# A long convolution and an MLP in one kernel: the engine and the place of batch 0's intermediate stores

## The chip, the core and the metric

One core of one Trainium2 chip runs the whole kernel. The metric is device microseconds of one execution; before the change the median of three runs is 1598.55 us (1595.64 to 1606.63).

## What is computed

The reference is a gated long convolution (sequence 12480, 128 channels, batch 2) followed by a two-layer MLP with a leaky ReLU:

```python
h_filt = (np.maximum(pos_emb @ w1, 0.0) @ w2) * np.exp(-0.01 * pos)[:, None]
u = x * v
Hf = np.fft.rfft(h_filt, n=L, axis=0)            # L = 2 * S
y = np.fft.irfft(np.fft.rfft(u, n=L, axis=1) * Hf[None], n=L, axis=1)[:, :S, :]
t = (x * y).reshape(B * S, D)
h = t @ w_in                                     # 128 -> 2048
out = np.maximum(0.01 * h, h) @ w_out            # 2048 -> 128
```

## The kernel before

The transform is cut as 98 times 128 points, so that each part is a matmul. The work has three stages, and on each engine the instructions run in the order in which the program writes them (`manual_schedule`).

**First stage** (to about 142 us; lines 265 to 409). For 16 groups of positions SyncE loads the transform's factors, x and v; TensorE does the 98-point transform of batch 0 and of the filter's hidden layer; the results go to the DRAM scratch `scr1`. Every DMA of this stage is started by SyncE.

**Second stage** (about 142 to 312 us; lines 697 to 885), batch 0. A loop over 25 chunks of four frequencies each (`KC` = 4, `NCH` = 25; the last frequency chunk has two) goes in the order `ORD`: chunks 13 to 24, then 12, then 0 to 11. Below, i is the place in this order, and "chunk 18" means i = 18. Iteration i does:

- `load_b` (line 705): SyncE loads the data of chunk i+3 (768 KB, four buffers `bin`);
- matmuls `hp` (line 846), and two ScalarE copies into `hs` (line 850): the filter's spectrum of this chunk (tile `hs`, two buffers);
- `fwd` (line 135): the forward transform `up`; then `hidden(i+1)` (line 790), copied by ScalarE into `es` (line 793);
- `store_h` (line 815): two DMAs of 256 KB that put `hs` into the DRAM scratch `hspec`, from where batch 1's work reads it in the third stage (`fetch_h`, line 489). ScalarE starts them;
- up to five steps of `weights` (line 708): eight rounds of three iterations turn the float64 weights into pairs of float32r. Integer work on VectorE (lines 80 to 91) reads the raw tiles `wi64` and `wo64`; the next round's loads (lines 717 and 718, 256 KB each) stand in iterations 3, 6, ..., 21, and the first instruction that reads the loaded tile (line 80) comes in the same iteration, behind the product;
- `product` (lines 143 and 144): four VectorE multiplications of `up` with `hs` and two sums, one of them on GpSimd (in the last two iterations both on VectorE);
- for chunk i-1: the back transform `dp` (line 163), two ScalarE copies into `ct` (line 238; two buffers), and `store_back` (line 220): one DMA of 512 KB to the scratch `scr2`, started by ScalarE (for the last chunk by SyncE). For the last two chunks `last_c` (line 657) also copies four short rows straight from `ct` into `cin[0]`, the input of the third stage's first tile.

Also in this loop, on SyncE: `first_c` (reads of `scr2` for tile 0) in iterations 15 to 19; `fetch_a(0)` and `fetch_a(1)` (lines 246 to 256: seven DMAs, 1.4 MB, for batch 1's first transform) in iterations 20 and 23; `load_gx(0)` and `load_gx(1)` (lines 605 to 620, six DMAs) in iterations 23 and 24; `rows_c` (line 650) in iteration 24, which reads rows of `scr2` up to those of chunk 22. `mult_a` (line 262) multiplies what `fetch_a` brought, on GpSimd.

Behind the loop come `ahead(1)` (four steps of `conv`, the generator of batch 1's transforms, whose first step stands before the loop), the rest of `weights`, the last chunk's back transform, and `join_hi(0)`, `upper_c(1)` and `rows_c(1, ...)`: the loads of tile 1's `cin`.

**Third stage** (to the end; lines 888 to 1248). Tiles of 390 positions of the output are joined, back-transformed, gated and put through the MLP, in 49 blocks of 16 steps (`NF` = 16); batch 1's transforms (`conv`) run between. `steps` is a table written out before the loop: at step i of the third stage, `do` runs what is due there ("piece" at step 2, "mult" at 9, loads and joins by the tables `gets` and `turn_at`). Join work of tile 1 is due at steps 2 to 4. Pools `s0` (tags s0, s1: three buffers each) and `sc` (tag s4: two buffers) are used from the first stage to the third by `fetch_a`, by batch 1's chunks and by `conv`'s output `o1`.

A DMA is started by an instruction on the queue of SyncE (SPq) or of ScalarE (ACTq); in the views it is a row DMA_DIRECT2D of that queue, and while it waits, everything behind it on the same engine waits too.

Of the kernel before, what the change touches and what calls it, by code (L numbers as in the profile page):

```python
# [8 lines left out]
F32 = mybir.dt.float32  # L9
# [21 lines left out]
def tile_conv_mlp(ctx, tc, x, v, pos_emb, w1, w2, w_in, w_out, cf, cr, cg, cb, ci, cw, out):  # L31
# [78 lines left out]
    def run(g):  # L110
        for _ in g:
            pass
# [105 lines left out]
    def store_back(b, c, ct, eng):  # L218
        k0, n = chunk(c)
        eng.dma_start(out=scr2[b][k0:k0 + n].rearrange("k r m e -> (r m) k e"),  # L220
                          in_=ct[:, :n].rearrange("p k s d -> p k (s d)"))
# [20 lines left out]
    with tc.manual_schedule():  # L242
# [175 lines left out]
        wc_l = wp.tile([128, D], F32R, name="wc_l")  # L418
        sc = ctx.enter_context(tc.tile_pool(name="sc", bufs=2, reuse_waits="tile"))
        psc = {}  # L420
        N1 = HB // MC1
        WAIT = 12
        PRE = 2
# [273 lines left out]
        with ExitStack() as st:  # L697
# [97 lines left out]
            def evac(c):  # L795
                ct = sbb.tile([128, KC, 2, D], F32, tag="ct", name="ct", bufs=2)
                k0, n = chunk(c)
                end = c == ORD[-1]
                dp = dps.pop(c)
                if end:  # L800
                    for s, copy in ((0, nc.scalar.copy), (1, nc.vector.tensor_copy)):
                        copy(ct[:, :n, s, :], dp[s][:, :n * D].rearrange("p (k d) -> p k d", d=D))
                else:
                    run(back_evac(dp, ct, n))
                if c in ORD[-2:]:
                    last_c(ct, k0, n, [nc.sync] * 3 + [nc.scalar if end else nc.sync])
                store_back(0, c, ct, nc.sync if end else nc.scalar)

            def store_h(c, hs, i):

                w = chunk(c)[1] * D

                def put(eng):
                    for s in range(2):
                        eng.dma_start(out=hspec[c][:, :, s, :w], in_=hs[HB * s:HB * s + HB, :, :w])
                put(nc.scalar)

            eh, dps = {}, {}
            first_c = upper_c(0)
            ahead(A0)  # L820
            next(conv)
            hidden(ORD[0])
            for i, c in enumerate(ORD):
                if i + 3 < NCH:
                    load_b(ORD[i + 3])
                if NCH - 10 <= i < NCH - 5:
                    next(first_c)
                if i == NCH - 2:
                    load_gx(0)
                if i == NCH - 1:  # L830
                    load_gx(1)
                    rows_c(0, 0, 0, (MID - 2) * KC)
                if i in FETCH:
                    fetch_a(FETCH.index(i))
                if i == NCH - 2:
                    mult_a(0)
                for f in late:
                    f()
                late = []
                n = chunk(c)[1]  # L840
                t, es = bins.pop(c), eh.pop(c)
                hp = two("h")
                for ri in range(2):
                    for k in range(n):
                        h, j = 64 * (k % 2), ri * n // 2 + k // 2
                        nc.tensor.matmul(hp[k % 2][:, D * j:D * j + D], es[h:h + 64, k // 2, ri, :], w22[h:h + 64, :],
                                         start=True, stop=True)
                hs = sbb.tile([128, 2, KC // 2, 2, D], F32, tag="hs", name="hs", bufs=2)
                for k in range(2):
                    nc.scalar.copy(hs[:, :, :n // 2, k, :],  # L850
                                   hp[k][:, :n * D].rearrange("p (r j d) -> p r j d", r=2, d=D))
                hs = hs.rearrange("p r j i d -> p r (j i d)")
                up = two("u")
                fwd(up, lambda s: t[:, :n, s, FO:], n)
                if i + 1 < NCH:
                    hidden(ORD[i + 1])
                store_h(c, hs, i)
                for _ in range(3):
                    next(wprep, None)
                pins[c] = sbb.tile([128, 2, 512], F32, tag="pin", name="pin", bufs=2)  # L860
                ab = [sbb.tile([128, 2, 512], F32, tag=g, name=g) for g in ("ta", "tb")]
                product(ab, up, hs, n * D, pins[c], nc.vector if i >= NCH - 2 else nc.gpsimd)
                if i >= 1:
                    b4 = ORD[i - 1]
                    dps[b4] = two("d")
                    back_halves(dps[b4], pins.pop(b4), b4)
                    evac(b4)
                for _ in range(2):
                    next(wprep, None)

            def flush():
                for f in late:
                    f()
                late.clear()

            ahead(1)
            run(wprep)
            mult_a(1)
# [1 line left out]
            back_halves(dps[ORD[-1]], pins.pop(ORD[-1]), ORD[-1])  # L880
            evac(ORD[-1])
            run(join_hi(0))
            run(upper_c(1))
            rows_c(1, 0, 0, KH)
            psc["held"] = []
# [278 lines left out]
                at(0, "load", t)  # L1164

        at(2, "piece", 0)
        at(9, "mult", PRE)

        def do(what, t, i):
            if what == "piece":  # L1170
                run(pieces_out.pop(0))
                for f in psc.pop("held"):
                    f()
                fetch_a(PRE)
            elif what == "mult":
                mult_a(t)
            elif what == "conv":
# [139 lines left out]
```

## Time and profile before

| | us |
|---|---|
| median of three runs | 1598.55 |
| the runs | 1598.55, 1595.64, 1606.63 |
| the profiled execution | 1601.6 |
| its span | 1599.7 |
| TensorE busy (matmuls) | 1555.3 (97%) |
| VectorE busy | 1138.7 (71%) |
| ScalarE busy | 998.1 (62%) |
| GpSimd busy | 767.0 (48%) |

The span is what the profiler saw between the first and the last instruction; the execution's own time has 1.9 us more around it. Times in the rows are counted from the span's start. Shares of the whole span say little here, as the three stages have different limits, and only the second stage and its end are touched by the change.

### The profile page before, as it was taken

How to read it: one execution, taken by the hardware profiler on the slowest of the kernel's cores; microseconds unless marked ns; L12 is line 12 of the kernel's file. 1: busy time of each engine (PE TensorE's matmuls, PEld its weight loads, DVE VectorE, ACT ScalarE, POOL GpSimd, SP SyncE). 2: the span in 40 equal slices, each digit the busy share in tenths (PEclk: the TensorE clock that was granted, in tenths of full speed). 3: DMA queues.
4: the chain of work that ended last, by engine and by line, in shares of the span. 5: the costliest groups of instructions: out<-in, count | busy, mean ns of one | idle time of the engine just before them, and what ended most of it. 6: DMA issues, size and time to landing. Idle time of an engine off the chain costs nothing.

```text
span 1599.7 us, 27485 instructions
## 1 busy us (share of the span) xinstructions
PE 1555.3 (97%) x9241; PEld 1322.6 (83%) x9241; DVE 1138.7 (71%) x1785; ACT 998.1 (62%) x2108; POOL 767.0 (48%) x806
## 2 busy tenths in 40 slices
PE   7888999899999999999999999999999999999998
PEld 7887555588889888888888888988888888888888
DVE  6874888756975566666676765677777777777776
ACT  2332555346664477777777776667777676777776
POOL 6772122146654275867776873633443433334310
PEclk9999999999999999999999999999999999999999
DMA  9998999767767477657556650421212212121200
GB/s 268 304 307 283 320 318 340 243 198 203 222 198 216 136 194 192 197 162 197 173 160 181 171 153 32 138 85 55 69 54 68 80 57 89 56 61 59 64 11 21
DMA packets 166268, 253.30 MB, mean 158 GB/s; under 512 B 14240, under 2 KB 118932, under 8 KB 163056
## 3 DMA queue, kind: packets, MB, share of 16 engines
q1 hardware_dynamic: 146388, 226.28, 47.7%
q10 hardware_dynamic: 19740, 25.28, 4.5%
q8 instruction: 73, 1.20, 0.3%
q14 instruction: 67, 0.55, 0.1%
HBM read 168.03 MB, written 83.43 MB: 157 GB/s over the span
## 4 chain that ended last, share of the span: by engine, by line
PE 75%; DMA 11%; DVE 8%; ACT 2%; issue 2%; POOL 1%; SPq 1%; ACTq 0%; DVEq 0%; POOLq 0%
PE mh L1009 29%; PE acc L1051 9%; PE acc L1052 9%; PE acc L1050 9%; PE yp L932 4%; PE cv L149 3%; DMA scr<-o 3%; PE cv L445 3%; DMA scr<-ct 2%; DMA ft<-in_cf_dram 2%; PE op L1082 2%; PE a L398 2%; PE zp L951 1%; PE up L135 1%; DVE ta L143 1%
## 5 line engine op out<-in xcount | busy, mean ns | idle before, releaser
L1014 DVE SCALAR_TENSOR_TENSOR rl<-mh,rh 128x512 fp32r<-128x512 f32 (+1 forms) x336 | 226.7, 682 | 198.7 <-ACT rh L1013 197.4
L1022 DVE TENSOR_TENSOR rl<-mh,rh 128x512 fp32r<-128x512 f32 (+2 forms) x416 | 277.4, 670 | 83.6 <-ACT rh L1021 75.1
L1017 ACT ACTIVATE mh<-mh 128x512 f32<-128x512 f32 (+2 forms) x416 | 236.9, 570 | 153.8 <-PE mh L1009 143.5
L1009 PE MATMUL mh<-zh,w_in_h 128*128 128x512 f32 (+3 forms) x800 | 315.9, 395 | 3.8 <-DVE rl L1014 2.6
L1009 PE MATMUL mh<-zl,w_in_h 128*128 128x512 f32 (+3 forms) x800 | 299.2, 374 | 0.3 <-POOL zl L965 0.2
L1051 PE MATMUL acc<-rl,w_out_h 128*128 128x512 f32 (+3 forms) x800 | 299.1, 374 | 0.1
L1050 PE MATMUL acc<-rh,w_out_h 128*128 128x512 f32 (+3 forms) x800 | 299.0, 374 | 0.0
L1052 PE MATMUL acc<-rh,w_out_l 128*128 128x512 f32 (+3 forms) x800 | 299.0, 374 | 0.0
L1009 PE MATMUL mh<-zh,w_in_l 128*128 128x512 f32 (+3 forms) x800 | 299.0, 374 | 0.0
L1013 ACT ACTIVATE rh<-mh 128x512 fp32r<-128x512 f32 (+1 forms) x336 | 199.1, 596 | 136.8 <-PE mh L1009 128.4
L965 POOL TENSOR_TENSOR zl<-zf,zh 128x390 fp32r<-128x390 f32 (+24 forms) x110 | 67.7, 628 | 395.7 <-ACT zh L964 371.0
L687 POOL TENSOR_TENSOR cp<-cq,cp 98x256 f32<-98x256 f32 x248 | 194.1, 783 | 29.3 <-DVE cp L675 12.6
L1019 DVE CAST rh<-mh 128x512 fp32r<-128x512 f32 (+2 forms) x208 | 139.5, 671 | 65.6 <-ACT mh L1017 65.3
L1009 PEld LDWEIGHTS mh<-zh,w_in_h 128*128 128x128 f32 x800 | 151.2, 189 | 30.1 <-DVE rl L1014 9.2
L1051 PEld LDWEIGHTS acc<-rl,w_out_h 128*128 128x128 f32 x800 | 151.2, 189 | 20.2 <-DVE rl L1022 0.4
L1050 PEld LDWEIGHTS acc<-rh,w_out_h 128*128 128x128 f32 x800 | 151.2, 189 | 19.8
L1052 PEld LDWEIGHTS acc<-rh,w_out_l 128*128 128x128 f32 x800 | 151.2, 189 | 19.7
L1009 PEld LDWEIGHTS mh<-zh,w_in_l 128*128 128x128 f32 x800 | 151.2, 189 | 19.7
L1009 PEld LDWEIGHTS mh<-zl,w_in_h 128*128 128x128 f32 x800 | 151.6, 190 | 15.9 <-POOL zl L965 0.6
L1021 ACT CAST rh<-mh 128x512 fp32r<-128x512 f32 (+2 forms) x208 | 118.7, 571 | 6.7
L684 POOL TENSOR_TENSOR cq<-cin 98x256 f32<-98x256 f32 x124 | 97.3, 784 | 0.9 <-DMA cin<-scr 0.8
L144 POOL TENSOR_TENSOR pin<-ta,tb 128x512 f32<-128x512 f32 (+1 forms) x23 | 28.8, 1253 | 130.7 <-DVE tb L143 130.7
(168 smaller groups left out, 2559.3 us busy)
## 6 DMA issues: line engine op xcount, KB each, us to landing
cin<-scr SPq DMA_DIRECT2D x318, 98.0 KB
hd<-hspec SPq DMA_DIRECT2D x48, 512.0 KB
bin<-scr SPq DMA_DIRECT2D x24, 768.0 KB
scr<-o SPq DMA_DIRECT2D x28, 588.0 KB
scr<-ct SPq DMA_DIRECT2D x25, 512.0 KB
scr1b<-o SPq DMA_DIRECT2D x32, 392.0 KB
hspec<-hs ACTq DMA_DIRECT2D x48, 256.0 KB
xm<-in_x_dram SPq DMA_DIRECT2D x128, 96.0 KB
```

The lines of the kernel that those rows point to most:

```text
L684: eng.tensor_tensor(out=cq[:, p], in0=ci_t[:, 0, :, 0, :], in1=ci_t[:, 0, :, 1, :], op=op)
L687: eng.tensor_tensor(out=cp[:, p, w], in0=cq[:, p], in1=cp[:, p, 1], op=op)
L1009: nc.tensor.matmul(hp, u[:, fs], m, start=(i == 0), stop=(i == 2))
L1013: nc.scalar.activation(out=split2(rh), in_=plain(hp), func=AF.Relu)
L1014: nc.vector.scalar_tensor_tensor(out=split2(rl), in0=plain(hp), scalar=0.0, in1=split2(rh), op0=ALU.max, op1=ALU.subtract)
L1017: nc.scalar.activation(out=hp, in_=hp, func=AF.Lrelu, alpha=0.01)
L1019: nc.vector.tensor_copy(split2(rh), plain(hp))
L1021: nc.scalar.copy(split2(rh), plain(hp))
L1022: nc.vector.tensor_tensor(out=split2(rl), in0=plain(hp), in1=split2(rh), op=ALU.subtract)
L1050: nc.tensor.matmul(ap, w_out_h[:, f, :], rh, start=(f == 0 and not sums(k)), stop=False)
L1051: nc.tensor.matmul(ap, w_out_h[:, f, :], rl, start=False, stop=False)
L1052: nc.tensor.matmul(ap, w_out_l[:, f, :], rh, start=False, stop=(f == NF - 1))
```

## The change

The stores of the filter's spectra (`store_h`) and of the back transforms (`store_back`, but for the last chunk, which SyncE started already) are put into a list `late` that SyncE's queue runs at the head of the next iteration, before that iteration's `load_b`; ScalarE starts none of them. A `flush` behind the loop runs what is left: the last chunk's spectrum and chunk 23's back transform.

For i = 19 to 22 (`KEEP`) the spectrum isn't put into the two rotating buffers `hs` but into buffers of the long-lived pools: two in one buffer of tag s4, one in s1, one in s0 (`place_h`). Their stores are kept: two run behind `join_hi(0)`, ahead of tile 1's loads, the other two at steps 6 and 7 of the third stage, behind what the table has at these steps. `conv`'s first step, which takes the other s4 buffer, moves from before the loop to i = 19. No arithmetic changes.

```diff
--- before.py
+++ after.py
@@ -418,6 +418,7 @@
         wc_l = wp.tile([128, D], F32R, name="wc_l")
         sc = ctx.enter_context(tc.tile_pool(name="sc", bufs=2, reuse_waits="tile"))
         psc = {}
+        kept = []
         N1 = HB // MC1
         WAIT = 12
         PRE = 2
@@ -804,7 +805,29 @@
                     run(back_evac(dp, ct, n))
                 if c in ORD[-2:]:
                     last_c(ct, k0, n, [nc.sync] * 3 + [nc.scalar if end else nc.sync])
-                store_back(0, c, ct, nc.sync if end else nc.scalar)
+                if end:
+                    store_back(0, c, ct, nc.sync)
+                else:
+                    late.append(lambda: store_back(0, c, ct, nc.sync))
+
+            KEEP = range(NCH - 6, NCH - 2)
+            pair = []
+
+            def place_h(i):
+
+                j = i - KEEP[0]
+                if i not in KEEP:
+                    return sbb.tile([128, 2, KC // 2, 2, D], F32, tag="hs", name="hs", bufs=2)
+                if j < 2:
+                    if j == 0:
+                        pair.append(sc.tile([128, 2048], F32, tag="s4", name="hs2"))
+                        next(conv)
+                    t = pair[0][:, 1024 * j:1024 * j + 1024]
+                elif j == 2:
+                    t = s0.tile([128, 1024], F32, tag="s1", name="hs1", bufs=3)
+                else:
+                    t = s0.tile([128, MC1 * 4 * NA], F32, tag="s0", name="hs0", bufs=3)[:, :1024]
+                return t.rearrange("p (r j i d) -> p r j i d", r=2, j=KC // 2, d=D)
 
             def store_h(c, hs, i):
 
@@ -813,14 +836,18 @@
                 def put(eng):
                     for s in range(2):
                         eng.dma_start(out=hspec[c][:, :, s, :w], in_=hs[HB * s:HB * s + HB, :, :w])
-                put(nc.scalar)
+                if i in KEEP:
+                    kept.append(lambda: put(nc.sync))
+                else:
+                    late.append(lambda: put(nc.sync))
 
             eh, dps = {}, {}
             first_c = upper_c(0)
-            ahead(A0)
-            next(conv)
             hidden(ORD[0])
             for i, c in enumerate(ORD):
+                for f in late:
+                    f()
+                late = []
                 if i + 3 < NCH:
                     load_b(ORD[i + 3])
                 if NCH - 10 <= i < NCH - 5:
@@ -834,9 +861,6 @@
                     fetch_a(FETCH.index(i))
                 if i == NCH - 2:
                     mult_a(0)
-                for f in late:
-                    f()
-                late = []
                 n = chunk(c)[1]
                 t, es = bins.pop(c), eh.pop(c)
                 hp = two("h")
@@ -845,7 +869,7 @@
                         h, j = 64 * (k % 2), ri * n // 2 + k // 2
                         nc.tensor.matmul(hp[k % 2][:, D * j:D * j + D], es[h:h + 64, k // 2, ri, :], w22[h:h + 64, :],
                                          start=True, stop=True)
-                hs = sbb.tile([128, 2, KC // 2, 2, D], F32, tag="hs", name="hs", bufs=2)
+                hs = place_h(i)
                 for k in range(2):
                     nc.scalar.copy(hs[:, :, :n // 2, k, :],
                                    hp[k][:, :n * D].rearrange("p (r j d) -> p r j d", r=2, d=D))
@@ -873,6 +897,7 @@
                     f()
                 late.clear()
 
+            flush()
             ahead(1)
             run(wprep)
             mult_a(1)
@@ -880,6 +905,8 @@
             back_halves(dps[ORD[-1]], pins.pop(ORD[-1]), ORD[-1])
             evac(ORD[-1])
             run(join_hi(0))
+            for f in kept[:2]:
+                f()
             run(upper_c(1))
             rows_c(1, 0, 0, KH)
             psc["held"] = []
@@ -1164,6 +1191,8 @@
                 at(0, "load", t)
 
         at(2, "piece", 0)
+        at(6, "kept", 2)
+        at(7, "kept", 3)
         at(9, "mult", PRE)
 
         def do(what, t, i):
@@ -1172,6 +1201,8 @@
                 for f in psc.pop("held"):
                     f()
                 fetch_a(PRE)
+            elif what == "kept":
+                kept[t]()
             elif what == "mult":
                 mult_a(t)
             elif what == "conv":
```

## Rows read from the trace of the kernel before

**Rows 1.** Windows of 10 us: stretch and length, busy us of each engine, clock, DMA, GB/s
```profile
100.00:110.00 10.00, 9.58 (x64) 9.26 (x63) 8.89 (x17) 3.27 (x7) 8.67 (x5) 1.00 0.93 336
...
240.00:250.00 10.00, 9.79 (x80) 5.49 (x78) 7.94 (x16) 5.32 (x12) 2.55 (x2) 1.00 0.98 335
...
260.00:270.00 10.00, 9.79 (x88) 5.90 (x86) 7.82 (x17) 5.18 (x12) 2.55 (x2) 1.00 1.01 353
...
290.00:300.00 10.00, 7.03 (x48) 3.40 (x46) 8.51 (x16) 4.61 (x9) 4.03 (x2) 0.83 0.87 250
```

**Rows 2.** Timeline of TensorE: the forward transforms of chunks 15, 18, 19 and 24
```profile
242.50 1.94 PE L135 MATMUL up<-bin,mb 128*64 128x512 f32 x8 [0.21 <-DVE ta L143]
...
260.72 1.94 PE L135 MATMUL up<-bin,mb 128*64 128x512 f32 x8 [0.21 <-DVE ta L143]
...
266.92 1.94 PE L135 MATMUL up<-bin,mb 128*64 128x512 f32 x8
...
304.22 1.94 PE L135 MATMUL up<-bin,mb 128*64 128x512 f32 x8 [1.59 <-DVE ta L143]
```

**Rows 3.** Timeline of ScalarE and its DMA issues in the late chunks
```profile
271.86 1.08 ACT L238 COPY ct<-dp 128x512 f32<-128x512 f32 x2 [1.49 <-PE dp L163]
...
285.25 1.08 ACT L238 COPY ct<-dp 128x512 f32<-128x512 f32 x2 [0.83 <-PE dp L163]
291.19 0.37 ACTq L220 DMA_DIRECT2D scr<-ct  x1
...
299.71 4.16 ACTq L815 DMA_DIRECT2D hspec<-hs  x2
```

**Rows 4.** Lines 815 and 657: ns of one issue (min/median/max), first and last start
```profile
L815 ACTq DMA_DIRECT2D hspec<-hs x50: 515/516/1186, 156.6 to 308.1; - x50
...
L657 SPq DMA_DIRECT2D cin<-ct x6: 572/572/1017, 310.8 to 315.8; - x6
```

**Rows 5.** Timeline of SyncE's DMA issues in chunks 23 and 24 and at the end
```profile
292.03 0.32 SPq L249 DMA_DIRECT2D ft<-in_cf_dram  x1
...
301.34 1.59 SPq L609 DMA_DIRECT2D gt<-in_cg_dram  x2
...
305.39 0.42 SPq L620 DMA_DIRECT2D xm<-in_x_dram  x1
308.39 1.04 SPq L650 DMA_DIRECT2D cin<-scr  x2
310.05 6.33 SPq L657 DMA_DIRECT2D cin<-ct  x7
```

**Rows 6.** Timeline of SyncE's DMA issues in the third stage: load_gx, then fetch_a
```profile
347.15 0.62 SPq L609 DMA_DIRECT2D gt<-in_cg_dram  x2
...
349.34 0.42 SPq L620 DMA_DIRECT2D xm<-in_x_dram  x1
350.88 0.33 SPq L249 DMA_DIRECT2D ft<-in_cf_dram  x1
...
354.60 0.57 SPq L69 DMA_DIRECT2D xv<-in_v_dram  x1
```

**Rows 7.** Timeline behind the stage: joins of tile 0 and tile 1
```profile
317.81 0.43 DVE L684 TENSOR_TENSOR cq<-cin 98x256 f32<-98x256 f32 x1 [2.63 <-DMA cin<-ct]
...
322.91 0.73 POOL L675 TENSOR_TENSOR cp<-cin 98x256 f32<-98x256 f32 x1 [0.54 <-DMA cin<-scr]
...
326.83 0.42 DVE L687 TENSOR_TENSOR cp<-cq,cp 98x256 f32<-98x256 f32 x1
```

**Rows 8.** Timeline of a raw weight's first use (chunk 18), of a load, and of its use
```profile
267.62 0.28 DVE L80 TENSOR_SCALAR fa<-wi 128x256 uint32<-128x256 uint32 x1
...
281.51 0.36 SPq L717 DMA_DIRECT2D wi<-in_moe_w_in_dram  x1
...
288.76 0.29 DVE L80 TENSOR_SCALAR fa<-wi 128x256 uint32<-128x256 uint32 x1 [1.45 <-DMA wi<-in_moe_w_in_dram]
```

**Rows 9.** The page's 40 slices of 40 us: GB/s of the DMA engines
```profile
GB/s 268 304 307 283 320 318 340 243 198 203 222 198 216 136 194 192 197 162 197 173 160 181 171 153 32 138 85 55 69 54 68 80 57 89 56 61 59 64 11 21
```


## Prediction

> **What bounds the kernel now.** I read the windows of the second stage first, then TensorE's timeline to see where its chunks fall behind, then the queues of ScalarE and SyncE at those places. In the windows the reader sees a stage in which everything is nearly full: near 240 us TensorE is busy 9.79 of 10 us and the DMA engines carry 335 GB/s at a share of 0.98, near 260 us 353 GB/s at 1.01 [rows 1]. Between 290 and 300 us TensorE falls to 7.03 of 10. TensorE paces the stage as long as it is fed: three chunks, from the transform of chunk 15 to that of chunk 18, take 260.72 - 242.50 = 18.22 us, 6.07 each [rows 2]. At that pace chunk 24 would begin at 260.72 + 6 x 6.07 = 297.2; it begins at 304.22. So 7.0 us are lost between chunks 18 and 24. A part of them is the clock, whose mean is 0.83 in the window in which TensorE idles [rows 1]; it goes with its cause.
>
> The cause is in ScalarE's queue [rows 3]. The copies of `ct` end at 285.25 + 1.08 = 286.33, but the store behind them is issued only at 291.19: ScalarE stands 4.9 us at the store, and the copies to `hs` that TensorE's work waits for stand behind it. At 299.71 two spectrum stores take 4.16 us to issue; one takes 0.52 at the median [rows 4]. A full DMA system holds up a compute engine, because that engine starts the stores.
>
> **The change, part by part.**
>
> *Stores off ScalarE, four spectra later.* ScalarE no longer stands at a store, and four chunks put 4 x 0.524 = 2.10 MB less through the DMA engines in the very stretch that is held; at 320 GB/s that is 6.6 us of DMA time. Both speak to the same 7.0 us, so they aren't added: -7.0 at most. Elsewhere the 1.4 us of issue per chunk that leave ScalarE (2 x 0.52 + 0.37) are worth nothing, as it is busy 5.32 of 10 us beside TensorE's 9.79 [rows 1, 3, 4].
>
> *What is late next: SyncE at the end of the stage.* SyncE used to run ahead in chunks 22 to 24, for its loads waited for little. Now its queue is tied to the back transforms: in iteration 23 it has chunk 21's `store_back` before `load_gx(0)`, and that waits for `ct`, copied in iteration 22. By the row of iteration 19, `ct` is done 271.86 + 1.08 - 266.92 = 6.0 us after the iteration's transform starts [rows 2, 3]. Without the loss chunk 22 starts at 260.72 + 4 x 6.07 = 285.0, so SyncE gets past the store at 291.0 + 0.4 = 291.4. Then, in order: `load_gx` took 301.34 to 305.81 = 4.5 us in the crowded stretch and 347.15 to 349.76 = 2.6 us in the third stage; `fetch_a` took 292.03 to 301.34 = 9.3 crowded, 350.88 to 355.17 = 4.3 free [rows 5, 6]. I take 3.5 and 6.5, near the middle, as the stretch has fewer bytes but its loads are now squeezed behind 291 us. That gives 301.4. Iteration 24: chunk 23's spectrum 1.2 (two issues with the step between them), chunk 22's `store_back` 0.4, `load_gx(1)` 3.5, `rows_c` 1.0, chunk 23's four short rows at 0.57 = 2.3 [rows 4, 5]: 309.8. The new `flush`: 1.2 + 0.4, 311.4. The last chunk's three short rows: 1.7, to 313.1. Before, they were all issued by 310.05 + 6.33 = 316.38, and the first join had its data at 317.81 [rows 5, 7]. I add 0.7 for the flushed megabyte in front of them in the same queue. The join then starts 316.4 - 313.1 - 0.7 = 2.6 us earlier, not 7.0: +4.4 given back. With all the free durations the same sum ends at 309.1, when the compute (297.2 plus the 12.2 us from 304.22 to 316.38) is as late: nothing given back. With the crowded ones it ends at 317.9: +8.5, or 1.5 us later than now.
>
> Beside this I hold a rule of the Trainium skill, DMA: Bandwidth & Descriptors, section Queues, rings and completion order: within one queue each DMA engine takes its descriptors in order, while it goes round between queues. By it the short rows would stand behind the whole flush, 1.05 MB, 3.3 us at 320 GB/s as an estimate, instead of my 0.7, and the sum below would end at +1.0 instead of -1.6. In the trace of before the two queues shared the work and the short rows landed 1.4 us after their issue; it doesn't show the case.
>
> *One queue instead of two, in chunks 2 to 18.* SyncE waits for the transform there for most of each chunk, so "a chunk late" is hardly late: `hs` and `ct` are done when it comes to them, or soon after. But `load_b` and the weights' loads now stand behind a store that waits for `ct`, some 4 us later than before. `load_b` is three chunks ahead: no cost. A raw weight isn't: by the 6.0 us above and the two issues in front it is started about 0.7 us after the transform of its own iteration, in chunk 18 near 261.4, and VectorE reads it at 267.62, 6.2 us later [rows 2, 8]. In the crowded stretch a load started at 281.51 was late: its reader began at 288.76, 7.25 us behind, having waited 1.45. If each of the seven loads is late by that 1.0 it costs 7 us, since VectorE and TensorE pace each other here; if the stores in front have drained, 0. Nor do I know whether one queue carries what two do: the chunks need 0.786 + 0.524 + 0.524 + 0.175 MB (the last a third of a round's weights) = 2.01 MB in 6.07 us = 331 GB/s, and one window of the first stage, with one queue only, shows 336 GB/s at a share of 0.93 [rows 1]. Ends: 0, and at 310 GB/s 6.48 us a chunk, 17 x 0.41 = +7.0. I take +1.0, near the row of 336.
>
> *Behind the stage.* Two kept chunks add four issues (2.1 us) and 1.05 MB (3.3 us at 320 GB/s) ahead of tile 1's loads. Tile 1's upper join ended at 322.91 + 0.73 = 323.64 and was needed at 326.83: 3.2 us of cover [rows 7]. Delay 2.1 to 5.0, cost 0 to 1.8; I take 0, the issue time having the nearer row. The other two stores stand behind the loads of their step, which the table starts ahead of their use: 0, up to 1.
>
> Sum: -7.0 + 4.4 + 1.0 + 0 = -1.6 us. The profiled execution took 1601.6, so 1600.0; it stands 3.05 above the median, so I predict 1597.0.
>
> **The rivals.**
>
> *All of the loss goes.* SyncE's loads run at the free durations, and the queue keeps up: -7.0, 1601.6 - 7.0 - 3.05 = 1591.5. For it: fewer bytes in the crowded stretch, and SyncE's own waits there cost no compute engine anything. Against: some 22 us of SyncE's issues now start at 291.
>
> *Slower: one queue is the bound from chunk 2.* If one queue carries less than the chunks want, every chunk stretches, `hs` and `ct` wait for their stores, the raw weights land late. At 310 GB/s: +7.0 - 7.0 + 4.4 = +4.4, 1603.0. It turns slower where the 17 chunks lose more than the 2.6 us gained at the end: 0.15 us each, below 2.01 / 6.22 = 323 GB/s. For it: the first four slices, with one queue for nearly all of that time, carry 268, 304, 307 and 283 GB/s [rows 9]. Against: the window of 336 GB/s, which had DMA share to spare.
>
> *The kept stores eat the rest.* Tile 1's loads are 5.0 us late and cost 1.8: +0.2, 1598.8, no change.
>
> **How the numbers follow.** The forecast has 0.40 (its own range 1594 to 1600.5), all of the loss 0.20, one queue 0.28, the kept stores 0.12. A range from 1589 to 1606 reaches through the first and the second rival and leaves out about 0.15. A measurement of this kernel can tell about 1%, 16 us, from no change. A gain of 16 us is more than twice the loss that the trace shows, and 16 us slower would need 281 GB/s through all 17 chunks (17 x 1.09 us). So within 1% 0.94, faster 0.02, slower 0.04.
>
> **What would show it right or wrong.** Right: chunk 24's transform starts near 298 to 300, ScalarE has no stall at a store, and SyncE's last short rows are issued 2 to 4 us earlier than 316.38, with the first join waiting for them. The one-queue rival shows as chunks of 6.3 us or more between 170 and 260 us, and as waits of line 80 for `wi`; the kept-stores rival as tile 1's join starting later behind the stage's end than now. Wrong altogether: a change over 8 us either way, or one that comes from the third stage.

## The result, and the profile after

The changed kernel is slower: 1620.66 us (median of six, 1615.82 to 1625.07) against 1599.02, ratio 1.0132, 95% interval 1.0109 to 1.0156, so about 21 us. The profiled execution took 1620.04 us, its span is 1617.9 (before 1599.7).

TensorE's timeline cuts the 18.2 us more of span at three marks: the forward transforms of chunks 0 and 24, and the first back transform of tile 0 (`yp`), which opens the third stage.

| us | before | after | more |
|---|---|---|---|
| start to chunk 0 | 152.79 | 152.17 | -0.6 |
| chunk 0 to chunk 24 | 151.42 | 156.20 | +4.8 |
| chunk 24 to the first `yp` | 14.62 | 21.15 | +6.5 |
| from there to TensorE's end | 1277.35 | 1284.88 | +7.5 |

Rows after the change, on TensorE's timeline. The first two, the transforms of chunks 18 and 24, answer [rows 2]; the last two are tile 2's back transform:

```profile
265.62 1.94 PE L135 MATMUL up<-bin,mb 128*64 128x512 f32 x8 [0.20 <-DVE ta L143]
...
308.37 1.94 PE L135 MATMUL up<-bin,mb 128*64 128x512 f32 x8 [1.46 <-DVE ta L143]
...
329.51 1.48 PE L1008 MATMUL yp<-cp,gt 98*64 98x128 f32 x8 [6.61 <-DVE cp L688]
...
376.39 0.87 PE L959 MATMUL yp<-cp,gt 98*64 98x128 f32 x10
380.39 0.65 PE L959 MATMUL yp<-cp,gt 98*64 98x128 f32 x6 [3.12 <-POOL cp L688]
```

Against [rows 2] chunk 18 starts 4.9 us later and chunk 24 4.2 us later, and TensorE stands 6.6 us at the end of the stage and 3.1 us in the third. The three parts have three causes.

**The stage.** VectorE's waits after the change (us in total, times, longest), between 150 and 310 us; before, the line reads 1.4, 1, 1.4:

```profile
DVE fa L80 <- DMA wi<-in_moe_w_in_dram: 7.6, 5, 2.1
```

The raw weights come late in five of eight rounds. On SyncE's timeline the reader sees why: the weights (L718) stand behind `store_back` (L220), which waits for the copies of `ct`, so the weights start only at 247.44, 1.7 us behind the transform of chunk 15 (245.73), and VectorE's first read of them (254.28, on its timeline) waits 1.59 us.

```profile
245.51 0.36 SPq L220 DMA_DIRECT2D scr<-ct  x1
245.97 0.46 SPq L706 DMA_DIRECT2D bin<-scr  x1
246.53 0.82 SPq L630 DMA_DIRECT2D cin<-scr  x1
247.44 0.36 SPq L718 DMA_DIRECT2D wi<-in_moe_w_in_dram  x1
...
254.28 0.29 DVE L80 TENSOR_SCALAR fa<-wi 128x256 uint32<-128x256 uint32 x1 [1.59 <-DMA wi<-in_moe_w_in_dram]
...
313.99 7.46 SPq L658 DMA_DIRECT2D cin<-ct  x4
321.50 1.22 SPq L838 DMA_DIRECT2D hspec<-hs  x2
322.76 0.69 SPq L220 DMA_DIRECT2D scr<-ct  x1
323.57 3.27 SPq L658 DMA_DIRECT2D cin<-ct  x3
...
327.37 3.58 SPq L838 DMA_DIRECT2D hspec<-hs  x4
...
355.22 3.06 SPq L838 DMA_DIRECT2D hspec<-hs  x4
358.37 1.66 SPq L610 DMA_DIRECT2D gt<-in_cg_dram  x2
...
368.82 0.32 SPq L249 DMA_DIRECT2D ft<-in_cf_dram  x1
```

**The end of the stage.** Four short rows take 7.46 us to issue, then the two flushed stores (321.50, 322.76) go ahead of the last chunk's rows, which are issued by 326.84; in [rows 5] they were issued by 316.38. The waits of SyncE's queue name the hold:

```profile
SPq L658 <- DMA cin<-ct: 4.9, 1, 4.9
```

A DMA start waits for a `cin` row that another DMA brings. The records of the DMA instructions tell which. Each DMA of either queue signals its landing on one of eight semaphores (101 to 108, counters that instructions can wait for); the numbers go round over both queues together, and a start waits until the DMA that had its number before has landed. ScalarE's one short row, of chunk 24, holds number 108, between SyncE's 107 (309.75) and 101 (310.23); SyncE's next start with 108 is the fourth row of chunk 23:

```
start   us    engine line  tiles        waits for   own
309.75  0.44  SP     L616  xm<-in_x     107         107
310.23  0.63  SP     L618  xm<-in_x     101         101
315.38  0.57  SP     L658  cin<-ct      107         107
319.01  1.20  ACT    L658  cin<-ct      99          108
320.88  0.57  SP     L658  cin<-ct      108         108
```

ScalarE's row lands at 320.86, and the next start with its number follows at 320.88. So chunk 23's row waits for a row of chunk 24. Tile 0's join, which answers the first of [rows 7], has its data at 328.49 instead of 317.81:

```profile
318.16 0.69 DVE L803 COPY ct<-dp 128x512 f32<-128x512 f32 x1 [0.68 <-PE dp L163]
...
328.49 0.42 DVE L685 TENSOR_TENSOR cq<-cin 98x256 f32<-98x256 f32 x1 [8.97 <-DMA cin<-ct]
```

The first row is the last copy of `ct`, from which the last chunk's rows are taken. Before, it stood here:

```profile
313.82 0.69 DVE L802 COPY ct<-dp 128x512 f32<-128x512 f32 x1 [0.50 <-PE dp L163]
```

From the end of this copy to the join it took 3.3 us before and takes 9.6 us after: 6.3 us more, nearly all of the +6.5 in the table.

**Behind the stage.** Windows of 10 us, the first two before and the last two after the change (columns as in [rows 1]; the clock is the third number from the end):

```profile
320.00:330.00 10.00, 8.65 (x56) 6.78 (x55) 7.98 (x20) 3.60 (x9) 1.46 (x2) 1.00 0.57 186
330.00:340.00 10.00, 9.52 (x68) 8.68 (x69) 5.76 (x12) 3.98 (x10) 6.70 (x9) 1.00 0.78 208
...
320.00:330.00 10.00, 3.39 (x31) 3.12 (x31) 1.45 (x4) 1.17 (x2) 0.00 (x0) 0.88 0.62 177
330.00:340.00 10.00, 9.30 (x39) 7.53 (x39) 5.40 (x14) 2.22 (x7) 1.46 (x2) 0.50 0.60 189
```

After TensorE's 6.6 us of idling the clock stands at 0.50, the lower of its two levels (1.2 GHz), for a whole window: the third stage goes from 10.7 us late to 13.6. Then the kept stores of steps 6 and 7 (355.22 above) move SyncE's line: `fetch_a` starts at 368.82 instead of 350.88 [rows 6], 18 us late where the matmuls were 13.6 late. GpSimd's product of what it fetches stands ahead of tile 2's join, in GpSimd's timeline:

```profile
377.31 2.34 POOL L262 TENSOR_TENSOR xv<-xv,xv 98x1024 f32<-98x1024 f32 x1 [13.93 <-DMA xv<-in_v_dram]
379.61 0.72 POOL L688 TENSOR_TENSOR cp<-cq,cp 98x256 f32<-98x256 f32 x1
```

### The profile page after: what moved, and what is told of

Same layout as the page of the kernel before. It is cut to its first block, busy times and chain, and to the rows that moved or that the text cites. A ratio compares the mean times of both kernels' runs of the same rounds, so it can differ in the third digit from the quotient of the medians.

```text
span 1617.9 us, 27520 instructions
## 1 busy us (share of the span) xinstructions
PE 1566.2 (97%) x9241; PEld 1334.0 (82%) x9241; DVE 1142.0 (71%) x1785; ACT 994.6 (61%) x2108; POOL 762.4 (47%) x806
## 4 chain that ended last, share of the span: by engine, by line
PE 72%; DMA 11%; DVE 9%; ACT 2%; issue 2%; POOL 2%; SPq 2%; DVEq 0%; ACTq 0%; POOLq 0%
PE mh L1036 28%; PE acc L1078 9%; PE acc L1079 9%; PE acc L1077 9%; PE yp L959 4%; PE cv L149 3%; DMA ft<-in_cf_dram 3%; PE cv L446 2%; DMA wi<-in_moe_w_in_dram 2%; PE op L1109 2%; PE zp L978 1%; DMA scr<-o 1%; PE up L135 1%; DMA cin<-scr 1%; DVE ta L143 1%
```

## The experiments

All beside runs of the kernel before on the same chip. The columns to the right are of the profiled execution, cut at the marks of the first table, minus before. Single profiles differ by some us there: E12, whose code is that of before up to tile 1's rows, has -0.4 and +1.6 in the first two, so the ratio decides.

| kernel | median us | ratio (95%) | chunk 0 to 24 | 24 to `yp` | rest |
|---|---|---|---|---|---|
| the change | 1620.66 | 1.0132 (1.0109 to 1.0156) | +4.8 | +6.5 | +7.5 |
| E1 kept, others by ScalarE | 1611.05 | 1.0056 (1.0036 to 1.0076) | -2.8 | +1.5 | +8.0 |
| E2 all by SyncE, none kept | 1615.13 | 1.0084 (1.0052 to 1.0116) | +7.3 | +6.3 | +3.4 |
| E3 loads ahead of stores | 1611.15 | 1.0067 (1.0044 to 1.0089) | -1.0 | +4.9 | +7.6 |
| E4 last short row on SyncE | 1619.22 | 1.0091 (1.0059 to 1.0124) | +0.3 | +4.5 | +7.8 |
| E5 E1, two kept later | 1611.64 | 1.0067 (1.0042 to 1.0092) | -3.1 | +1.5 | +13.3 |
| E6 E3 + E4, four kept later | 1610.38 | 1.0056 (1.0036 to 1.0076) | -0.7 | +4.2 | +7.7 |
| E7 before, products on VectorE | 1600.94 | 1.0009 (0.9993 to 1.0025) | -1.9 | +1.5 | -0.1 |
| E8 E1 + E7, four kept later | 1606.40 | 1.0029 (1.0011 to 1.0048) | -3.3 | +1.5 | +10.2 |
| E9 E8, kept never stored | 1601.00 | 1.0002 (0.9985 to 1.0019) | -3.6 | +1.5 | +3.7 |
| E10 E8, kept by ScalarE | 1608.26 | 1.0033 (1.0016 to 1.0050) | -4.9 | -0.3 | +10.6 |
| E11 E6, flush behind rows, kept by ScalarE | 1613.57 | 1.0072 (1.0049 to 1.0096) | -2.9 | +4.0 | +9.3 |
| E12 before + eight small loads | 1605.50 | 1.0019 (1.0001 to 1.0038) | -0.4 | +1.6 | +8.8 |
| E13 E11, kept never stored | 1603.45 | 1.0020 (1.0001 to 1.0038) | -1.2 | +1.3 | +4.3 |
| E14 the change, kept never stored | 1614.88 | 1.0084 (1.0064 to 1.0105) | +2.9 | +7.0 | +4.4 |

### The two halves of the change alone (E1, E2)

```diff
-  late.append(lambda: store_back(0, c, ct, nc.sync))      # E1, against the change
+  store_back(0, c, ct, nc.scalar)
-      late.append(lambda: put(nc.sync))
+      put(nc.scalar)
-  KEEP = range(NCH - 6, NCH - 2)                          # E2; kept stores gone,
+  KEEP = range(NCH - 6, NCH - 6)                          # conv's first step where it was
```

> Keeps the four spectra but lets ScalarE start all other stores at once, as before the change. Theory S (SyncE's order is the loss): the waits of line 80 for wi go (0 instead of 7.6 us), chunk 24's transform starts at 298 to 303, the first join at 312 to 317; only the kept stores' 3 us in the third stage may stay: 1592 to 1600 us. Rival K (the kept stores are the loss): still 1612 us or more, with the same stall of the third stage near 370 us. Rival Q (one queue carries less than two): as S, 1592 to 1600.

> Keeps nothing back: SyncE starts all stores, one iteration late, and no store runs behind the stage. Theory S: the waits of line 80 for wi stay (4 to 8 us up to chunk 20), the end of the stage is at least as late as in the changed kernel, the third stage loses its 3.5 us stall: 1613 to 1625 us. Rival K: 1597 to 1604 us. Rival Q: 1620 us or more, since 2.1 MB come back to the one queue in the crowded stretch.

Each half alone costs: 0.56% and 0.84%. E1 fits neither theory, as S had at most 1600 and K at least 1612 for it; E2 is where S had it. With ScalarE at the stores and less of them (E1) the stage gains 2.8 us, not 7.0: chunk 24 still waits 5.1 us, and the timelines of GpSimd, VectorE and TensorE of E1 show what ScalarE's stall had hidden.

```profile
289.07 2.80 POOL L262 TENSOR_TENSOR xv<-xv,xv 98x1024 f32<-98x1024 f32 x1
293.74 2.60 POOL L262 TENSOR_TENSOR xv<-xv,xv 98x1024 f32<-98x1024 f32 x1 [1.87 <-DMA gt<-in_cg_dram]
...
289.58 2.57 DVE L735 TENSOR_TENSOR w_in_l<-wi,w_in_h 128x256 fp32r<-128x256 f32 x1
...
294.17 2.45 DVE L90 SCALAR_TENSOR_TENSOR fb<-wo,fs 128x256 f32<-128x256 uint32 x1
...
299.76 3.68 PE L135 MATMUL up<-bin,mb 128*64 128x512 f32 x8 [5.12 <-DVE ta L143]
```

Both VectorE operations take 0.42 us elsewhere; beside GpSimd's product they end 0.3 us after it, 2 us later than alone. The trace of before has the like twice (2.80 and 2.38 at 296; 2.37 and, for a sum of 128x512, 2.66 at 304), which the prediction had passed over. In E2 the raw weights cost most (12.6 us of waits, one of 6.99), and SyncE's wait at the short rows is there again (4.5 us).

### Order and semaphore in SyncE's line (E3, E4)

```diff
-               for f in late:
-                   f()
-               late = []
                if i + 3 < NCH:                     # E3: late stores behind load_b
                    load_b(ORD[i + 3])              # and the raw weights' loads
...
-                    rows_c(0, 0, 0, (MID - 2) * KC)
...
+               stores, late = late, []
                store_h(c, hs, i)
-               for _ in range(3):
+               for n_ in range(3):
                    next(wprep, None)
+                   if n_ == 0:
+                       for f in stores:
+                           f()
+                       if i == NCH - 1:
+                           rows_c(0, 0, 0, (MID - 2) * KC)
-  last_c(ct, k0, n, [nc.sync] * 3 + [nc.scalar if end else nc.sync])   # E4
+  last_c(ct, k0, n, [nc.sync] * 4)
```

> The changed kernel with SyncE's late stores put behind the iteration's own loads (load_b and the raw weights) instead of ahead of them. Theory S: a raw weight is again loaded 9 us or more ahead of line 80, whose waits for wi fall from 7.6 us to under 1; chunk 20 starts near 273 instead of 278.6; 1613 to 1618 us, as the end of the stage stays. Rival Q: the waits move to other tiles (hs, ct, bin) and chunk 20 still starts at 277 or later.

> The changed kernel with the one short row of the last chunk that ScalarE starts put on SyncE, so that no DMA of SyncE can wait for one that ScalarE starts later. Theory S: chunk 23's four short rows are issued within 3 us instead of 7.5, the first join starts 4 to 5 us earlier (323 to 324 instead of 328.5), less time at the lower clock: 1611 to 1617 us. Rival Q (the rows stand behind the stores' bytes in the one queue): the first join moves by under 1.5 us, 1618 to 1622 us.

In E3 the weights start without a store in front (SyncE's timeline), 0.35 us ahead of the transform of chunk 15 (239.52), and the waits of line 80 fall from 7.6 to 2.7 us, not under 1 as expected; 0.65% comes back, more than was expected, and E3's interval lies below that of the change.

```profile
239.17 0.36 SPq L718 DMA_DIRECT2D wi<-in_moe_w_in_dram  x1
239.59 0.42 SPq L719 DMA_DIRECT2D wo<-in_moe_w_out_dram  x1
240.10 1.17 SPq L838 DMA_DIRECT2D hspec<-hs  x2
```

In E4 SyncE doesn't stand at chunk 23's rows (2.58 us for four, 7.46 in the change). The rows of SyncE, then those of VectorE with the last copy of `ct` and tile 0's join:

```profile
310.86 2.58 SPq L658 DMA_DIRECT2D cin<-ct  x4
313.49 1.21 SPq L838 DMA_DIRECT2D hspec<-hs  x2
314.75 0.68 SPq L220 DMA_DIRECT2D scr<-ct  x1
315.54 3.89 SPq L658 DMA_DIRECT2D cin<-ct  x4
...
313.73 0.69 DVE L803 COPY ct<-dp 128x512 f32<-128x512 f32 x1
...
320.76 0.42 DVE L685 TENSOR_TENSOR cq<-cin 98x256 f32<-98x256 f32 x1 [5.67 <-DMA cin<-ct]
```

The shared semaphore is shown by this: one row moved to the other queue, and the wait of 4.9 us is gone. What it is worth is read from the end of the copy to the join: 6.3 us in E4 against 9.6 in the change, so 3.3 us. The join's own time, 320.76 instead of 328.49, says less, for in this profile chunk 24 begins 5.7 us earlier too, which the edit doesn't touch; the profile is of the fastest of E4's four executions. In the time E4 hardly shows: its median (1619.22) lies in rival Q's range, and its interval overlaps that of the change.

The late rows take 3.89 us for four here. In E13 below, where the flush stands behind them, four take 2.41 (309.83 to 312.24) and the join comes 3.8 us behind the copy: the flush in front costs 2.5 us.

### What stalls ScalarE's neighbours (E7, E8)

```diff
-  def mult_a(c):                            # E7, on the kernel before
+  def mult_a(c, eng=nc.gpsimd):
-      nc.gpsimd.tensor_tensor(out=xt, in0=xt, in1=vt, op=ALU.mult)
+      eng.tensor_tensor(out=xt, in0=xt, in1=vt, op=ALU.mult)
-                    mult_a(0)
+                    mult_a(0, nc.vector)
-            mult_a(1)
+            mult_a(1, nc.vector)
-            for f in kept[:2]:              # E8: E1 + E7, the four kept stores
-                f()                         # behind tile 1's rows
             run(upper_c(1))
             rows_c(1, 0, 0, KH)
+            for f in kept[:4]:
+                f()
```

> The kernel before with one edit: the two products of the third stage's first inputs (L262) on VectorE instead of GpSimd. Theory V (about 4 of the 7 us that PE loses between chunks 18 and 24 are VectorE held while GpSimd multiplies): no VectorE row of 512 elements above 1 us near 296 and 304, chunk 24 starts 1 to 3 us earlier than 304.2 (VectorE has the two products to do itself), time 1595 to 1601. Theory S (the prediction's: all of it is ScalarE standing at its stores): chunk 24 not earlier than 303.7, or later by the products' own time, time 1599 to 1604.

> ScalarE begins the other stores at once, four kept and all put behind tile 1's short rows on SyncE, the two products on VectorE. If both stalls are real and both removals add (Theory V with P): no gap of PE above 2 us between chunks 18 and 24, first transform of tile 0 4 to 7 us earlier than 318.8, time 1593 to 1599. If VectorE only takes over the products' time (S) or the kept bytes cost wherever they stand (B): 1602 or more.

In E7's timelines the stretched rows are gone; VectorE does each product itself, the first in 1.22 us:

```profile
292.47 0.43 DVE L734 TENSOR_TENSOR w_in_l<-wi,w_in_h 128x256 fp32r<-128x256 f32 x1
...
293.34 1.22 DVE L262 TENSOR_TENSOR xv<-xv,xv 98x1024 f32<-98x1024 f32 x1
...
295.92 0.42 DVE L90 SCALAR_TENSOR_TENSOR fb<-wo,fs 128x256 f32<-128x256 uint32 x1
...
299.48 3.58 PE L135 MATMUL up<-bin,mb 128*64 128x512 f32 x8 [2.02 <-DVE ta L143]
```

From chunk 18 to 24 it takes 42.46 us instead of 43.49, so the collision is worth 1.0 us net (1.6 against E12, which does this stretch as before does and takes 44.05), and the time as a whole can't be told from before. It lies in the ranges of both theories; the rows speak for V, with a quarter of the 4 us that it had. With both stalls removed the stretch is 41.15 in E8, 40.64 in E9, 39.64 in E10: of the 7.0 us that the prediction read there, 2.3 to 3.9 come back. In E8 they are lost again behind the stage (1606.40, where V with P had at most 1599).

### What a kept store costs (E5, E9, E10, E12)

```diff
             run(upper_c(1))                 # E5: E1, two kept stores moved here
             rows_c(1, 0, 0, KH)
+            for f in kept[:2]:
+                f()
-  kept.append(lambda: put(nc.sync))         # E10: E8, begun by ScalarE
+  kept.append(lambda: put(nc.scalar))
+  dm = s0.tile([128, 8], F32, tag="dm", name="dm", bufs=1)   # E12: before,
+  for j in range(8):                        # behind rows_c(1, ...)
+      nc.sync.dma_start(out=dm[:NA, j:j + 1], in_=cf[:, 0, 0, j:j + 1])
```

E9 is E8 without the loop over `kept`, and with `hspec[ORD[0]]` read for those four chunks.

> The kernel in which ScalarE begins the other stores at once and four are kept (1611 us), with the first two kept stores put behind tile 1's short rows on SyncE, the other two unchanged. Theory P (what the kept stores cost is their place in SyncE's line: they hold tile 1's loads for 3.5 us and VectorE, PE and the clock after that): tile 1's step from +5.2 to under +1.5, first transform of tile 0 still 3 us early, time 1603 to 1608. Theory B (the kept megabyte costs by its bytes wherever it stands, since tile 1's loads share the DMA engines with it): the step stays at 4 or more, time 1609 to 1613.

> ScalarE begins the other stores at once, the two products on VectorE, and the four kept spectra are never stored (left out: their four stores; batch 1 reads chunk 0's stored spectrum in their place, the same bytes). It prices what the eight DMA starts behind the stage cost. Theory I (SyncE's line is full behind the stage, every start in it pushes the later loads by its own issue time): against the kernel that has the eight starts behind tile 1's rows (1606.4), tile 1's step of +4 and the third stage's +1.5 go, time 1596 to 1602. Theory N (the steps behind the stage have another source, the first loads shifted against GpSimd's products): steps of 3 us or more stay, time 1603 or more.

> As the kernel with four kept and two products on VectorE (1606.4), but ScalarE begins the eight kept stores, behind tile 1's rows, so SyncE's line is as before. Theory I (issue time in SyncE's line): SyncE's first third-stage load back within 1 us of its place relative to tile 1's rows, time 1598 to 1603; what is left is 8 x 0.57 = 4.6 us of ScalarE's issuing beside its own work. Theory B (bytes, wherever begun): 1605 or more.

> The kernel before with eight added loads of 98 x 4 bytes on SyncE behind tile 1's short rows (nothing reads them). Theory I (a DMA start in SyncE's line behind the stage costs its issue time, whatever it carries): the line moves by 8 x 0.6 = 5 us, a step of 2 to 6 us at tile 1 or in the third stage, time 1602 to 1608. Theory B (the kept megabyte's bytes are what costs): no step over 1 us, time 1598 to 1601.

E5 moved the price, it didn't remove it (1611.64, theory B's range): tile 1's step, which B would have kept, went, and tile 2's back transform then waited 5.8 us for GpSimd, as in the change. E9 against E8 gives a price: 1.0029 - 1.0002, 0.27% or 4.3 us, for eight starts on SyncE with their bytes. The two intervals overlap, but the profiles agree: on TensorE's timeline the last back transform of tile 1 and that of tile 2 start 25.7 us apart before and in E9, 30.5 in E8. E12 carries 392 bytes a start and costs 0.19%, 3 us; its eight starts take 3.35 us of SyncE's timeline:

```profile
318.33 3.35 SPq L887 DMA_DIRECT2D dm<-in_cf_dram  x8
```

This agrees with a price that goes with the starts and not with the bytes: time in SyncE's line, which before too issues almost without a break from 317 to 350 us, so that the later loads move with it. It isn't shown: E12's interval begins at 0.01%, and its profile has no step at tile 1, 1.5 us near 370 and 5 us near 455, far behind the added starts. A share of the bytes isn't excluded, as E9, E13 and E14 leave out starts and bytes together. Another way, that loads wait for the buffers which the kept spectra hold, isn't seen: in the change no start of SyncE behind the stage waits for a store of `hs`.

On ScalarE (E10) the eight starts are no cheaper. Rows of ScalarE, SyncE and TensorE:

```profile
309.50 13.99 ACTq L838 DMA_DIRECT2D hspec<-hs  x8
...
310.38 3.80 SPq L630 DMA_DIRECT2D cin<-scr  x3
...
325.18 0.69 PE L1036 MATMUL mh<-zh,w_in_h 128*128 128x390 f32 x1 [9.41 <-ACT zh L1023]
```

ScalarE and SyncE take the eight semaphores in turn, each stands until the other's DMA has landed, and TensorE waits 9.4 us for a cast that stands behind ScalarE's stores. The theory "SyncE's line as before" missed this, and so 1608.26 stands in the range of theory B without speaking for bytes.

### The change, mended and without the kept stores (E6, E11, E13, E14)

E6 is E3 and E4 with all of `kept` behind `rows_c(1, ...)`; E11 is E6 with two further edits; E13 and E14 leave the kept stores out of E11 and of the change, as E9 does.

```diff
-            flush()                         # E11, against E6
             ahead(1)
...
             evac(ORD[-1])
+            flush()
-  kept.append(lambda: put(nc.sync))
+  kept.append(lambda: put(nc.scalar))
```

> The change with SyncE still beginning every store, mended in three places: late stores behind the input and raw-weight loads of their chunk, the fourth short row of chunk 24 on SyncE, all four kept stores behind tile 1's short rows. Theory P (the loss of 21 us is order: what stands ahead of what in SyncE's line, and the semaphore that two engines share; the engine that begins the stores is harmless): first transform of tile 0 within 2 us of before, no wait of SyncE over 3 us at the short rows, no step above 2 us later, time 1597 to 1606. Theory B (one engine cannot begin all of it without loss): chunk 24 or the first transform 4 us or more late, time 1608 or more.

> SyncE begins the stores of the stage a chunk late as in the change, with the places mended: late stores behind the loads of their chunk, the two last late stores behind chunk 24's short rows, all short rows on SyncE, the four kept stores by ScalarE behind tile 1's rows. Theory P (order and SyncE's issue time explain the 21 us): first transform of tile 0 within 2 us of before, steps behind it under 3 us in sum, time 1597 to 1604. Theory B: 1607 or more, as with the earlier mended one (1610).

> SyncE begins all stores of the stage a chunk late in the mended order (behind the loads of their chunk, the last two behind chunk 24's short rows, all short rows on SyncE); the four kept spectra are never stored (left out; batch 1 reads chunk 0's in their place). It prices the move to SyncE without the kept stores. Theory P (in that order the move costs nothing, what the mended kernels still lost, 9 and 13 us, are the eight kept starts): 1598 to 1604. Theory R (a rest of the move stays: SyncE's line at the end of the stage, the lower clock behind it): 1605 to 1609.

> The changed kernel as it is, only the four kept spectra never stored (left out; batch 1 reads chunk 0's in their place). It prices the eight kept starts where the change has them. Theory I (each start costs SyncE's issue time, 4 to 9 us for the eight): 1611 to 1616, third stage flat, the wait at the short rows still there. Theory O (behind a stage end that is already 10 us late the kept starts are hidden): 1618 or more.

E6 and E11 stayed at 1610 and 1614, where the theory of order alone had 1597 to 1606. For E11, E13 shows why: without its kept stores it is at 1.0020, so they cost E11 0.52% (8 us, on ScalarE; they start from 312.53 on, among SyncE's last short rows, with numbers of the same eight semaphores). E6 has its flush ahead of the rows besides, and wasn't run without the kept stores. In the right order the move of all other stores to SyncE costs 0.2% with an interval that begins at 0.01%. The timelines of SyncE and, for the last copy of `ct` and the join, VectorE at the end of E13's stage show that order:

```profile
305.86 6.38 SPq L658 DMA_DIRECT2D cin<-ct  x8
312.29 0.45 SPq L220 DMA_DIRECT2D scr<-ct  x1
312.79 1.50 SPq L838 DMA_DIRECT2D hspec<-hs  x2
314.33 1.08 SPq L220 DMA_DIRECT2D scr<-ct  x1
...
309.07 0.69 DVE L803 COPY ct<-dp 128x512 f32<-128x512 f32 x1 [0.47 <-PE dp L163]
...
313.56 0.42 DVE L685 TENSOR_TENSOR cq<-cin 98x256 f32<-98x256 f32 x1 [3.13 <-DMA cin<-ct]
```

E14 prices the kept stores in the change itself: 1.0132 - 1.0084, 0.48% or about 8 us, the two intervals just apart. Its profile has the stage's end as late as the change's, and tile 2's wait of 3.1 us is gone; the third stage isn't flat, as expected, but 4.4 us longer than before instead of 7.5. So 3.1 us of the 8 are seen at a place.

So the 21 us are: stores ahead of the weights (0.65% back in E3), a semaphore shared with ScalarE's last row (0.41% back in E4, not clear of noise, 3.3 us in the rows), the kept stores (0.48% back in E14), and in the rows 2.5 us for the flush ahead of the last short rows. E13 takes all four away and stands at 0.20%, so together they are 1.12% of the 1.32%. The three single prices add to 1.54%; within their intervals that is no more than the whole. None of these kernels beat the one before; E7, and E9 with four spectra left out, equal it.

## Why the prediction was wrong

Forecast 1597.0, 1589 to 1606; measured 1620.7. The forecast's terms were -7.0 (chunks 18 to 24), +1.0 (one queue), +4.4 (the stage's end) and 0 (behind it). The two profiles have -0.7 (42.75 us instead of 43.49), +5.5, +6.5 and +7.5 at these places.

- **"-7.0 at most", all of it given to ScalarE's stall: the size failed.** Even taking away both ScalarE's stall and VectorE's collision (E8 to E10) returned only 2.3 to 3.9 us from chunk 18 to 24. The pace of three quiet chunks, carried to chunk 24, was too fast a measure: GpSimd's products hold VectorE twice by 2 us, and by the code VectorE makes the last two chunks' sums alone (what this costs wasn't run). The 2.38 and 2.66 us rows stood in the trace of before. The Trainium skill (SBUF — State Buffer, Who interferes with whom) says that VectorE and GpSimd share a pair of ports under an exclusive lock, and that a VectorE instruction with two inputs in SBUF contends with a GpSimd instruction that reads SBUF; the rows agree (2.57 us beside 2.80, ending within 0.3 us). In E7 the collision is worth only 1.0 us net.
- **"A full DMA system holds up a compute engine, because that engine starts the stores": the stall is there, its cause is a semaphore too.** In the records of before, ScalarE's store at 291.19 has number 106; the DMA that had it last, ScalarE's own spectrum store of 283.96, landed at 291.12. In the 4.16 us of two spectrum stores the second (303.35) has number 105, which SyncE's load of `v`, started at 294.56, held until 303.32. So ScalarE stood for the landing of one earlier DMA, once of the other queue, and a start that moves to SyncE takes such a wait along.
- **"One queue instead of two": the mechanism was named, the term was mis-sized.** "If each of the seven loads is late by that 1.0 it costs 7 us" stood there with +1.0 taken. Line 80 waited 7.6 us in all, and chunks 0 to 18 took 113.45 us instead of 107.93, +5.5. The load was forecast to start 0.7 us behind its transform; in chunk 15 it was 1.7, with a read for tile 0 (246.53) in front as well. The rival's own mechanism (one queue carries less) is not what happened: the changed kernel's 40 us slices from 160 us carry 295 and 321 GB/s where [rows 9] have 320 and 318, and E3, with the same queue in another order, has no loss to chunk 24.

```profile
GB/s 257 305 317 287 295 321 293 192 207 229 211 202 216 155 156 212 175 189 177 168 168 179 192 144 59 117 88 58 76 58 63 70 62 87 58 63 62 63 10 21
```

- **"SyncE at the end of the stage", +4.4 against bounds of 0 to +8.5.** Chunk 24 to the first `yp` grew by 6.5 with chunk 24 itself not early, so the rows came 10 us late. The sum held the issues one by one, but not the wait of 4.9 us at a semaphore, worth 3.3 us: the working took a start to wait only for its own data. Its +4.4 came from an early chunk 24, so that E4 too has +4.5 there is chance. The flush was sized well: 1.6 us of issue and 0.7 for its bytes, 2.3, where the rows have 2.5. The rule that the prediction held beside this (the Trainium skill, DMA: Bandwidth & Descriptors, Queues, rings and completion order) would have put 1.6 and 3.3, 4.9 as an estimate; E4 against E13 doesn't bear that size out.
- **"Behind the stage", 0 for the kept stores: failed.** Measured about 8 us by the ratios (E14), 3.1 of them at tile 2. The cover of 3.2 us before tile 1's join was there, but the price isn't paid at that join: SyncE's line, full until 350 us, moves, and the wait appears at GpSimd's product and tile 2. "The other two stores stand behind the loads of their step: 0, up to 1" is the same mistake; at 355.22 they stand ahead of the next.
- **The clock** was left to "go with its cause". It came back as a cost: 0.50 in the window behind TensorE's 6.6 us of idling, where the delay grew from 10.7 to 13.6 us. E14, without the kept stores, loses the same 3 us there at a clock of 0.51.
- "16 us slower would need 281 GB/s through all 17 chunks" bounded one mechanism and gave slower by over 1% only 0.04. Four terms made it: no saving, one queue and the stage's end near their upper bounds (5.5 of 7.0, 6.5 of 8.5), and the third stage far above its own (7.5, where 1.8 and 1 were the ends).

## What to carry to other kernels

Moving a DMA start to an idle-looking engine moves it into a line: list what stands behind it there, and what each start waits for, the landing of earlier DMAs with the same semaphore included. Put stores that wait for results behind loads that others wait for (E3), and let one engine begin a group of DMAs that share a deadline (E4). A loss that is read as one stall should be tried without that stall before it is priced; the next cause often stands under it.

## What the runs showed that was not expected

- Eight semaphores for all DMAs of both queues couple the two engines: 4.9 us of SyncE for one row of ScalarE's (gone in E4), and 13.99 us for eight starts of ScalarE's in E10, where one takes 0.52.
- Starts on SyncE behind the stage seem to cost some 0.4 us each in the kernel's time (3 us for eight of 392 bytes, 4.3 for eight of 256 KB), though SyncE computes nothing; neither price is clear of noise.
- VectorE operations of 0.42 us took 2.4 to 2.6 us beside GpSimd's product of 98 x 1024 (E1).
